# A decode attention kernel: K and V loaded as 2 MB transfers with 16 KB per partition, V one group behind K, and weights loaded in long rows

## The chip, the cores and the metric

The kernel runs on one core of one Trainium2 chip. The metric is the device time of one execution in microseconds (us), the median of several. The profile is one more execution, recorded by the hardware profiler; its span, from the first to the last instruction, is 1.7 to 2.1 us shorter than the device time.

Names: TensorE (PE) multiplies matrices, and PEld is its weight load; VectorE (DVE), ScalarE (ACT) and SyncE (SP) are the other engines used. SP issues all of the DMA transfers but the five (before) or two (after) of w1 and w2. The profile counts 16 DMA engines for the core. SBUF is the memory, here tiles of 128 partitions, that the transfers fill; PSUM is the memory that TensorE writes its results to. In the records a load of all 128 partitions has 16 completions; here it has landed when the last of them has come (in the kernel before, TensorE's first matmul on a chunk comes 0.05 us after it at the earliest). A "packet" is one record of the DMA trace; for these loads it is one contiguous row of one partition (33,280 packets of 8 KB for 260 loads of 128 partitions, before).

## The reference, cut to what matters

One token, decoded: grouped-query attention over a long cache plus a small feed-forward block (FFN), everything in bf16.

```python
# x: [1,1,512]; k_cache, v_cache: [1, 8, 65536, 128]; wq: [512, 4096]; wo: [4096, 512]
# w1: [512, 1792]; w2: [1792, 512]
xn = _layernorm(x)
q  = (xn @ wq).reshape(1, 1, 32, 128)            # 32 heads, 4 per K/V group
scores = einsum("bhqd,bhkd->bhqk", q, repeat(k_cache, 4)) * 128 ** -0.5
o  = einsum("bhqk,bhkd->bhqd", softmax(scores), repeat(v_cache, 4))
out = x + o.reshape(1, 1, 4096) @ wo + (gelu(xn @ w1 + b1) @ w2 + b2)
```

K and V are 8 groups of 16 MB each: 256 MB that are read once. With the weights, the profile counts 280.5 MB (of 10^6 bytes) read from HBM.

## The kernel before

A group has 16 chunks of 4096 tokens (1 MB, 8 KB per partition). For a K chunk TensorE transposes 32 tiles into PSUM, VectorE and ScalarE copy them to SBUF, and 32 narrow matmuls give the scores. When a group's scores are complete, its maximum is found and ScalarE runs four exps, one for each head. A V chunk costs 32 narrow matmuls. V runs two groups behind K. The kernel turns all tile dependencies into semaphore waits.

```python
    NB = 12                                    # chunk buffers of 1 MB
    cbuf = [nc.alloc_sbuf_tensor(f"cbuf{i}", [128, TPC, DH], BF) for i in range(NB)]
    ...
    VLAG = 2
    for ph in range(NPH):                      # a phase: chunks of K of group ph, V of group ph - VLAG
        ks = [("K", ph, c) for c in range(NCH)] if ph < G else []
        vs = [("V", ph - VLAG, c) for c in range(NCH)] if ph >= VLAG else []
        ...                                    # taken in turn: K, V, K, V
    def item_src(it):
        kind, g, c = it
        cache = A_k_cache if kind == "K" else A_v_cache
        return cache[0, g, c * CH:(c + 1) * CH, :].rearrange("(p t) d -> p t d", p=128)
    ...                                        # SP issues each chunk's load as soon as its buffer is free
    def dma_w12():                             # issued by ACT after the last K chunk
        for kt in range(KT):
            ... in_=B_w1[kt * 128:(kt + 1) * 128, :]                    # rows of 3.5 KB
        ... in_=B_w2.rearrange("(fc p) n -> p fc n", p=128)             # rows of 1 KB
        # one semaphore: a reader of w1 waits for w1 and w2
    ...
        else:                                  # a V chunk
            if softmax_q and softmax_group[0] == g:
                flush_softmax()
            gen_pv(g, c, b)
            ...
            if ph == last_phase and pos_in_phase >= 1:
                for _ in range(ffn_per_item):  # 2 pieces of the FFN per V chunk
                    if ffn_pieces: ffn_pieces.pop(0)()
```

Of the kernel before, what the change touches and what calls it, by code (L numbers as in the profile page):

```python
# [5 lines left out]
BF = mybir.dt.bfloat16  # L6
# [144 lines left out]
def bass_parallel_sum__gqa_block_cached__dense_activation_gelu__decode_kernel(  # L151
# [13 lines left out]
    D = A_x.shape[-1]  # L165
    DH = 128
    H = A_wq.shape[1] // DH
    G = A_k_cache.shape[1]
    HPG = H // G
    S = A_k_cache.shape[2]  # L170
    F = B_w1.shape[1]
    FC = F // 128
    KT = D // 128
# [6 lines left out]
    assert D % 128 == 0 and F % 128 == 0 and S % CH == 0 and NCH % 4 == 0  # L180
    assert A_k_cache.shape[3] == DH and H % G == 0 and KT == 4 and HPG == 4

    NB = 12
    NKT = 4
    NPT = 4
    NPS = 2
    LA = 2

    SCALE = 1.0 / math.sqrt(DH)
    EPS = 1e-5  # L190
# [35 lines left out]
    finT = nc.alloc_sbuf_tensor("finT", [128, KT], F32)  # L226
    fin4_bf = nc.alloc_sbuf_tensor("fin4_bf", [KT, 128], BF)

    cbuf = [nc.alloc_sbuf_tensor(f"cbuf{i}", [128, TPC, DH], BF) for i in range(NB)]
    assert NB >= KT + 4 and TPC * DH == H * DH  # L230
    WQ_SLOT0 = NB - KT
    wq_kt = [cbuf[WQ_SLOT0 + kt][:, :, :].rearrange("p t d -> p (t d)") for kt in range(KT)]
    assert CH * NKT >= KT * F + FC * D
    R_kt = nc.alloc_sbuf_tensor("R_kt", [128, NKT * CH], BF)
    ktbuf = [R_kt[:, i * CH:(i + 1) * CH] for i in range(NKT)]
# [3 lines left out]
    wo_g = [nc.alloc_sbuf_tensor(f"wo_g{i}", [128, HPG, D], BF) for i in range(2)]  # L239
    scf = [nc.alloc_sbuf_tensor(f"scf{i}", [128, TPG * HPG], F32) for i in range(2)]  # L240
    scf_v = [scf[i][:, :].rearrange("p (t j) -> p t j", j=HPG) for i in range(2)]
    P_bf = [nc.alloc_sbuf_tensor(f"P_bf{i}", [128, TPG * HPG], BF) for i in range(3)]
    P_v = [P_bf[i][:, :].rearrange("p (t j) -> p t j", j=HPG) for i in range(3)]

    pmax = [nc.alloc_sbuf_tensor(f"pmax{i}", [128, HPG], F32) for i in range(2)]
    pmax_parts = [nc.alloc_sbuf_tensor(f"pmax_parts{i}", [128, BPG * HPG], F32) for i in range(2)]
# [54 lines left out]
    sch.dma(SP, lambda: sp.dma_start(out=b2row_bf[:, :], in_=B_b2.rearrange("(o n) -> o n", o=1)),  # L301
            sem_misc, writes=["b2row"], total=48)

    VLAG = 2
    NPH = G + VLAG
    items = []
    phase_start = []
    for ph in range(NPH):
        ks = [("K", ph, c) for c in range(NCH)] if ph < G else []
        vs = [("V", ph - VLAG, c) for c in range(NCH)] if ph >= VLAG else []  # L310
        phase_start.append(len(items))
        seq = []
        for c in range(NCH):
            if ks:
                seq.append(ks[c])
            if vs:
                seq.append(vs[c])
        items.extend(seq)
    NITEMS = len(items)
    assert NITEMS == 2 * NKCH  # L320
    NPB = VLAG + 1

    def item_src(it):
        kind, g, c = it
        cache = A_k_cache if kind == "K" else A_v_cache
        return cache[0, g, c * CH:(c + 1) * CH, :].rearrange("(p t) d -> p t d", p=128)

    next_item = [0]
    dma_hooks = {}

    def dma_items_upto(n_excl):
        while next_item[0] < min(n_excl, NITEMS):
            n = next_item[0]
            b = n % NB
            src = item_src(items[n])
            sch.dma(SP, lambda b=b, src=src: sp.dma_start(out=cbuf[b][:, :, :], in_=src),
                    csem[b], writes=[f"cbuf{b}"])
            for h in dma_hooks.get(n, ()):
                h()
            next_item[0] += 1  # L340

    def dma_wq():
        for kt in range(KT):
            sch.dma(
                SP,
                lambda kt=kt: sp.dma_start(out=wq_kt[kt], in_=A_wq[kt * 128:(kt + 1) * 128, :]),  # L346
                sem_wq, writes=[f"cbuf{WQ_SLOT0 + kt}"], total=16 * KT,
            )

    wo_sems = [sch.dsem("dwo0"), sch.dsem("dwo1")]  # L350
# [8 lines left out]
        )  # L359

    def dma_w12():
        for kt in range(KT):
            sch.dma(
                ACT,
                lambda kt=kt: act.dma_start(out=w1_sb[:, kt, :], in_=B_w1[kt * 128:(kt + 1) * 128, :]),
                sem_w12, writes=["w1_sb"] + (KT_RES_ALL if kt == 0 else []), total=16 * (KT + 1),
            )
        sch.dma(ACT, lambda: act.dma_start(out=w2_sb[:, :, :],
                                          in_=B_w2.rearrange("(fc p) n -> p fc n", p=128)),
                sem_w12, writes=["w2_sb"], total=16 * (KT + 1))  # L370

    dma_hooks[1] = [dma_wq]

    sch.op(DVE, lambda: dve.tensor_copy(out=xrow_f[:, :], in_=xrow_bf[:, :]),
           reads=["xrow_bf"], writes=["xrow_f"])
# [29 lines left out]
    for kt in range(KT):  # L405
        sch.op(
            PE,
            lambda kt=kt: pe.matmul(pA[:, PA_XN + kt:PA_XN + kt + 1],  # L408
                                    lhsT=xn_row_bf[0:1, kt * 128:(kt + 1) * 128],
                                    rhs=ident_bf[0:1, 0:1], start=True, stop=True),  # L410
            reads=["xn_row", "ident_bf"], writes=["pA"], publish=(kt == KT - 1),
        )
# [3 lines left out]
    def dva_for_fill(n):  # L416
        return DVE if (n % 8) in (0, 2, 3, 5, 6) else ACT

    def gen_transposes(i, b):
        for t in range(TPC):  # L420
            tg = i * TPC + t
            nfill = tg // 8
            tb = nfill % NPT
            slot = tg % 8
            last_of_bank = slot == 7
            sch.op(
                PE,
                lambda tb=tb, slot=slot, b=b, t=t: pe.transpose(  # L428
                    pst[tb][:, slot * 128:(slot + 1) * 128], cbuf[b][:, t, :], ident_bf[:, :]
                ),  # L430
                reads=[f"cbuf{b}", "ident_bf"], writes=[f"pst{tb}"], publish=last_of_bank,
            )
            if last_of_bank:
                e = dva_for_fill(nfill)
                kb = i % NKT
                q = t // 8
                dst = ktbuf[kb][:, q * 1024:(q + 1) * 1024]
                if e is DVE:
                    fn = (lambda tb=tb, dst=dst: dve.tensor_copy(out=dst, in_=pst[tb][:, :]))  # L439
                else:  # L440
                    fn = (lambda tb=tb, dst=dst: act.activation(out=dst, in_=pst[tb][:, :],  # L441
                                                                func=ACTF.Copy))
                sch.op(e, fn, reads=[f"pst{tb}"], writes=[f"ktbuf{kb}_{q}"])
# [80 lines left out]

    def gen_exps(g, js):
        gp = g % 2
        gq = g % 3
        for j in js:
            sch.op(
                ACT,  # L530
                lambda gp=gp, gq=gq, g=g, j=j: act.activation(  # L531
                    out=P_v[gq][:, :, j], in_=scf_v[gp][:, :, j], func=ACTF.Exp,
                    bias=negm[gp][:, j:j + 1], scale=1.0,
                    accum_out=sums[:, g * HPG + j:g * HPG + j + 1],
                ),
                reads=[f"negm{gp}"] + [f"scf{gp}_{k}" for k in range(BPG)],
                writes=[f"P{gq}_{j}", f"sums{g}_{j}"],
            )

    def gen_pv(g, c, b):  # L540
        gp = g % 3
        for t in range(TPC):
            sch.op(
                PE,
                lambda g=g, c=c, b=b, t=t, gp=gp: pe.matmul(  # L545
                    pB[:, PB_O + g * HPG:PB_O + (g + 1) * HPG],
                    lhsT=cbuf[b][:, t, :],
                    rhs=P_v[gp][:, c * TPC + t, :],
                    start=(c == 0 and t == 0), stop=(c == NCH - 1 and t == TPC - 1),
                ),  # L550
                reads=[f"cbuf{b}"] + [f"P{gp}_{j}" for j in range(HPG)], writes=["pB"],
                publish=(t == TPC - 1),
            )

    def gen_qproj():
        for h in range(H):
            for kt in range(KT):
                sch.op(
                    PE,
                    lambda h=h, kt=kt: pe.matmul(  # L560
                        pA[:, PA_Q + h:PA_Q + h + 1],
                        lhsT=wq_kt[kt][:, h * DH:(h + 1) * DH],
                        rhs=xnT_bf[:, kt:kt + 1], start=(kt == 0), stop=(kt == KT - 1),
                    ),
                    reads=[f"cbuf{WQ_SLOT0 + kt}", "xnT"], writes=["pA"],
                    publish=(h == H - 1 and kt == KT - 1),
                )
        sch.op(
            DVE,
            lambda: dve.tensor_scalar(out=qT_bf[:, :], in0=pA[:, PA_Q:PA_Q + H], scalar1=SCALE,  # L570
                                      scalar2=None, op0=ALU.mult),
            reads=["pA"], writes=["qT"],
        )
# [40 lines left out]
    def gen_ffn1_piece(fc):  # L614
        if True:
            for kt in range(KT):
# [1 line left out]
                    PE,  # L618
                    lambda fc=fc, kt=kt: pe.matmul(
                        pA[:, PA_H + fc:PA_H + fc + 1],  # L620
                        lhsT=w1_sb[:, kt, fc * 128:(fc + 1) * 128],
                        rhs=xnT_bf[:, kt:kt + 1], start=(kt == 0), stop=False,
                    ),
                    reads=["w1_sb", "xnT"], writes=["pA"], publish=False,
# [2 lines left out]
                PE,  # L627
                lambda fc=fc: pe.matmul(  # L628
                    pA[:, PA_H + fc:PA_H + fc + 1],
                    lhsT=b1row_bf[0:1, fc * 128:(fc + 1) * 128],  # L630
                    rhs=ident_bf[0:1, 0:1], start=False, stop=True,
                ),
                reads=["b1row", "ident_bf"], writes=["pA"], publish=(fc == FC - 1),
# [68 lines left out]
    ffn_per_item = -(-len(ffn_pieces) // max(1, NCH - 3))  # L702

    def dma_cap(n):
        return n if qproj_done[0] else min(n, NB - KT)

    dma_items_upto(dma_cap(NB))

# [20 lines left out]

    for n, it in enumerate(items):  # L730
        kind, g, c = it
        b = n % NB
        ph = phase_of_item[n]
        pos_in_phase = n - phase_start[ph]
        if kind == "K":
            i = kcount
            kcount += 1
            had_pending = bool(softmax_q)
            gen_transposes(i, b)
            if i == min(1, NKCH - 1):  # L740
                gen_qproj()
                qproj_done[0] = True
# [12 lines left out]
        else:  # L755
            if softmax_q and softmax_group[0] == g:
                flush_softmax()
            gen_pv(g, c, b)
            while epi_q:
                epi_q.pop(0)()  # L760
            if c == NCH - 1:
# [5 lines left out]
                        ffn_pieces.pop(0)()  # L767
        if pos_in_phase == min(6, NCH - 1) and ph >= VLAG:
            dma_wo(ph - VLAG)
        dma_items_upto(dma_cap(n + NB + 1))  # L770
    flush_softmax()
    while ffn_pieces:
        ffn_pieces.pop(0)()
# [77 lines left out]
```

## Time and profile before

| | before |
|---|---|
| time, median of 3 (lowest to highest) | 699.86 us (699.52 to 699.91) |
| span of the profile | 698.1 us |
| DMA share, 20 to 600 us | 1.01 in each stretch of 100 us |
| rate in those stretches | 408 to 416 GB/s |
| TensorE busy | 559.7 us (80%) |
| last V transfer landed | 692.8 us |

From the page of the kernel before, the lines that say how full the DMA engines are. In the row `DMA` each digit is the busy share of a fortieth of the span in tenths, 9 for 90% or more; the row below it is the rate.

```profile
DMA  8999999999999999999999999999999999999993
GB/s 344 418 416 415 416 416 417 415 412 416 416 415 413 416 416 416 416 412 417 417 416 411 406 418 416 418 400 411 417 417 417 380 416 416 416 413 400 411 392 139
DMA packets 44170, 282.22 MB, mean 404 GB/s; under 512 B 4379, under 2 KB 10269, under 8 KB 10782
q1 hardware_dynamic: 41678, 276.85, 96.7%
q8 instruction: 100, 1.64, 1.0%
DMA 58%; PE 36%; issue 3%; ACT 1%; DVE 1%; SPq 0%
```

The engines are busy from the first fortieth to the last but one. `q8`, which the page calls "instruction", is the fetch of instructions: 100 packets of 16 KB, 1.07 us each. The last line is the chain of work that ended last, by engine; "issue" is time in which an engine waited for nothing that the profile shows.

From the timeline of the kernel before, the end of the run on TensorE (start us, busy us, in brackets the idle time before):

```profile
692.88 1.02 PE L545 MATMUL pB<-P_bf,cbuf 128*128 128x4 bf16 x32 [1.50 <-DMA cbuf<-in_A_v_cache_dram]
693.76 0.57 PE L579 MATMUL pA<-sums,ones_f 128*128 128x4 f32 x2
```

After the last landing there are 32 matmuls and a short fixed tail; 692.8 to 698.1 is 5.3 us.

The trace also has a record of every DMA packet. Medians by size, counted from those records for the kernel before:

```
     4 B    4375 packets  median 9 ns      (semaphore updates)
  1024 B    5890 packets  median 46 ns     (wo, w2)
  3584 B     513 packets  median 140 ns    (w1)
  8192 B   33280 packets  median 313 ns    (K, V, wq)
```

A straight line through 1024 B and 8192 B, with 309 ns for the latter (its median from 5 to 15 us), has a slope of 27.2 B/ns and leaves about 8.5 ns per packet that does not depend on its size.

### The profile page before, as it was taken

What the parts mean: (1) busy time and instruction counts of PE and PEld (TensorE: products, weight loads), DVE (VectorE), ACT (ScalarE), POOL (GpSimd) and SP (SyncE); (2) the same over time, 40 slices, a digit from 0 to 9 for tenths busy, and PEclk for the clock granted to TensorE, in tenths of its full rate; (3) what the DMA queues carried; (4) which work ended last, traced back from release to release, by engine and by line L of the source; (5) the groups of instructions that cost most, each with busy time, mean ns of one, the idle gap of its engine ahead of it and who ended that gap; (6) DMA issues with size and microseconds to landing.
All of it is one profiled execution on the core that took longest, in us unless ns stands there. A gap on an engine that the chain in (4) does not pass through costs nothing.

```text
span 698.1 us, 26642 instructions
## 1 busy us (share of the span) xinstructions
PE 559.7 (80%) x12732; PEld 544.6 (78%) x12732; DVE 281.0 (40%) x457; ACT 245.1 (35%) x266; POOL 1.3 (0%) x10
## 2 busy tenths in 40 slices
PE   3888888998898888978888888989889979733454
PEld 3888888888898888878888888888888878633453
DVE  2366765444454444433444344544344434200000
ACT  4344664362335332352324422253323433300000
POOL 0000000000000000000000000000000000000000
PEclk9799999696778898785888687785788588655555
DMA  8999999999999999999999999999999999999993
GB/s 344 418 416 415 416 416 417 415 412 416 416 415 413 416 416 416 416 412 417 417 416 411 406 418 416 418 400 411 417 417 417 380 416 416 416 413 400 411 392 139
DMA packets 44170, 282.22 MB, mean 404 GB/s; under 512 B 4379, under 2 KB 10269, under 8 KB 10782
## 3 DMA queue, kind: packets, MB, share of 16 engines
q1 hardware_dynamic: 41678, 276.85, 96.7%
q10 hardware_dynamic: 2384, 3.67, 1.4%
q8 instruction: 100, 1.64, 1.0%
q14 instruction: 8, 0.07, 0.0%
HBM read 280.50 MB, written 0.00 MB: 402 GB/s over the span
## 4 chain that ended last, share of the span: by engine, by line
DMA 58%; PE 36%; issue 3%; ACT 1%; DVE 1%; SPq 0%
DMA cbuf<-in_A_k_cache_dram 41%; PE pst L428 23%; DMA cbuf<-in_A_v_cache_dram 15%; PE pss L454 7%; PE pB L545 4%; DMA cbuf<-in_A_wq_dram 2%; PE pA L560 1%; ACT R_kt L441 0%; PE pA L599 0%; PE pA L492 0%; PE pA L514 0%; SPq L346 0%; ACT P_bf L531 0%; PE pA L579 0%; ACT L531 0%
## 5 line engine op out<-in xcount | busy, mean ns | idle before, releaser
L428 PE MATMUL pst<-ident_bf,cbuf 128*128 128x128 bf16 x4096 | 331.8, 254 | 53.4 <-DMA cbuf<-in_A_k_cache_dram 37.5
L428 PEld LDWEIGHTS pst<-ident_bf,cbuf 128*128 128x128 bf16 x4096 | 305.8, 117 | 63.5 <-issue 57.6
L441 ACT ACTIVATE R_kt<-pst 128x1024 bf16<-128x1024 bf16 x192 | 196.3, 1024 | 358.3 <-PE pst L428 358.1
L439 DVE COPY R_kt<-pst 128x1024 bf16<-128x1024 bf16 x320 | 212.9, 688 | 259.6 <-PE pst L428 259.1
L545 PE MATMUL pB<-P_bf,cbuf 128*128 128x4 bf16 x4096 | 125.7, 165 | 54.9 <-DMA cbuf<-in_A_v_cache_dram 43.5
L545 PEld LDWEIGHTS pB<-P_bf,cbuf 128*128 128x128 bf16 x4096 | 115.5, 99 | 57.0 <-DMA cbuf<-in_A_v_cache_dram 44.1
L454 PE MATMUL pss<-qT_bf,R_kt 128*128 128x4 bf16 x4096 | 124.4, 165 | 6.3 <-issue 6.2
L454 PEld LDWEIGHTS pss<-qT_bf,R_kt 128*128 128x128 bf16 x4096 | 121.2, 98 | 7.0 <-issue 7.0
L531 ACT ACTIVATE P_bf<-scf,negm 128x512 bf16<-128x512 f32 x32 | 45.6, 1445 | 5.5 <-DVE negm L520 5.5
L471 DVE TENSOR_REDUCE pmax_parts<-scf 128x4 f32<-128x512 f32 x32 | 34.1, 1066 | 1.1
L467 DVE COPY scf<-pss 128x512 f32<-128x512 f32 x32 | 22.1, 692 | 22.1 <-PE pss L454 22.1
L583 DVE RECIPROCAL rtot<-pA 128x4 f32<-128x4 f32 x8 | 1.5, 183 | 65.3 <-PE pA L579 65.3
L646 ACT ACTIVATE g_t<-g_t 128x14 f32<-128x14 f32 x1 | 0.2, 214 | 62.6 <-DVE g_t L644 62.6
L599 PE MATMUL pA<-oT_bf,wo_g 128*128 128x1 bf16 x128 | 4.5, 165 | 5.2 <-DMA wo_g<-in_A_wo_dram 4.7
L609 DVE TENSOR_TENSOR finT<-pA,finT 128x4 f32<-128x4 f32 x8 | 1.3, 163 | 18.1 <-PE pA L599 18.1
L531 ACT ACTIVATION_READ_ACCUMULATOR P_bf<-scf,negm 128x1 f32 x32 | 8.4, 263 | 0.0
L599 PEld LDWEIGHTS pA<-oT_bf,wo_g 128*128 128x128 bf16 x128 | 4.0, 102 | 5.4 <-DMA wo_g<-in_A_wo_dram 4.8
L560 PE MATMUL pA<-xnT_bf,cbuf 128*128 128x1 bf16 x128 | 3.6, 165 | 5.1 <-DMA cbuf<-in_A_wq_dram 5.1
L560 PEld LDWEIGHTS pA<-xnT_bf,cbuf 128*128 128x128 bf16 x128 | 3.5, 104 | 5.3 <-DMA cbuf<-in_A_wq_dram 5.3
L637 DVE COPY h_f<-pA 128x14 f32<-128x14 f32 x1 | 0.2, 174 | 15.7 <-PE pA L628 15.7
L408 PE MATMUL pA<-ident_bf,xn_row_bf 1*128 1x1 bf16 x4 | 0.3, 164 | 7.6 <-ACT xn_row_bf L401 7.6
L408 PEld LDWEIGHTS pA<-ident_bf,xn_row_bf 1*128 1x128 bf16 x4 | 0.2, 101 | 7.6 <-ACT xn_row_bf L401 7.6
(62 smaller groups left out, 53.5 us busy)
## 6 DMA issues: line engine op xcount, KB each, us to landing
cbuf<-in_A_k_cache_dram SPq DMA_DIRECT2D x128, 1024.0 KB, 23.9
cbuf<-in_A_v_cache_dram SPq DMA_DIRECT2D x128, 1024.0 KB, 26.9
cbuf<-in_A_wq_dram SPq DMA_DIRECT2D x4, 1024.0 KB, 11.9
wo_g<-in_A_wo_dram SPq DMA_DIRECT2D x8, 512.0 KB, 27.0
R_kt<-in_B_w_dram ACTq DMA_DIRECT2D x4, 448.0 KB, 14.0
R_kt<-in_B_w_dram ACTq DMA_DIRECT2D x1, 1792.0 KB, 48.4
xrow_bf<-in_A_x_dram SPq DMA_DIRECT2D x1, 1.0 KB
b1row_bf<-in_B_b_dram SPq DMA_DIRECT2D x1, 3.5 KB
```

The costliest lines, as they stand in the source:

```text
L428: lambda tb=tb, slot=slot, b=b, t=t: pe.transpose(pst[tb][:, slot * 128:(slot + 1) * 128], cbuf[b][:, t, :], ident_bf[:, :]),
L439: fn = (lambda tb=tb, dst=dst: dve.tensor_copy(out=dst, in_=pst[tb][:, :]))
L441: fn = (lambda tb=tb, dst=dst: act.activation(out=dst, in_=pst[tb][:, :], func=ACTF.Copy))
L454: lambda sb=sb, slot=slot, kb=kb, t=t, g=g: pe.matmul(pss[sb][:, slot * HPG:(slot + 1) * HPG], lhsT=ktbuf[kb][:, t * 128:(t + 1) * 128], r ...
L467: sch.op(DVE, lambda sb=sb, dst=dst: dve.tensor_copy(out=dst, in_=pss[sb][:, :]), reads=[f"pss{sb}"], writes=[f"scf{gp}_{k4}"])
L471: lambda gp=gp, k4=k4, dst=dst: dve.tensor_reduce(out=pmax_parts[gp][:, k4 * HPG:(k4 + 1) * HPG], in_=dst.rearrange("p (t j) -> p j t", j= ...
L531: lambda gp=gp, gq=gq, g=g, j=j: act.activation(out=P_v[gq][:, :, j], in_=scf_v[gp][:, :, j], func=ACTF.Exp, bias=negm[gp][:, j:j + 1], sc ...
L545: lambda g=g, c=c, b=b, t=t, gp=gp: pe.matmul(pB[:, PB_O + g * HPG:PB_O + (g + 1) * HPG], lhsT=cbuf[b][:, t, :], rhs=P_v[gp][:, c * TPC + ...
L560: lambda h=h, kt=kt: pe.matmul(pA[:, PA_Q + h:PA_Q + h + 1], lhsT=wq_kt[kt][:, h * DH:(h + 1) * DH], rhs=xnT_bf[:, kt:kt + 1], start=(kt = ...
L583: sch.op(DVE, lambda hs=hs: dve.reciprocal(out=rtot[:, hs], in_=pA[:, PA_SUM:PA_SUM + HPG]), reads=["pA"], writes=[f"rtot{g}"])
L599: lambda kt=kt, j=j, h=h, g=g: pe.matmul(pA[:, PA_AT + kt:PA_AT + kt + 1], lhsT=wo_g[g % 2][:, j, kt * 128:(kt + 1) * 128], rhs=oT_bf[:, h ...
L609: lambda: dve.tensor_tensor(out=finT[:, :], in0=pA[:, PA_AT:PA_AT + KT], in1=finT[:, :], op=ALU.add),
```

## The change

The intent: K and V come in transfers of 2 MB whose rows are 16 KB per partition, in 8 buffers of 2 MB. V is one group behind K instead of two. The weights wq, w1 and w2 are laid out so that a partition reads one long row: partition p holds rows 4p to 4p+3 of w1 and rows 14p to 14p+13 of w2. For that, w1's columns are read by the matmuls with a step of 14 elements (28 bytes).

```diff
-    NB = 12
+    NSUB = 2
+    TPD = NSUB * TPC
+    NB = 8
...
+    VLAG = 1
+    NPB = VLAG + 1
...
-    cbuf = [nc.alloc_sbuf_tensor(f"cbuf{i}", [128, TPC, DH], BF) for i in range(NB)]
+    call = nc.alloc_sbuf_tensor("cbuf", [128, NB * TPD * DH], BF)
+    cbuf = [call[:, i * TPD * DH:(i + 1) * TPD * DH].rearrange("p (t d) -> p t d", d=DH)
+            for i in range(NB)]
...
+        for c in range(0, NCH + NSUB, NSUB):          # K K, then V V
+            if ph < G and c < NCH:
+                items.extend(("K", ph, c + s) for s in range(NSUB))
+            if ph >= VLAG and c >= NSUB:
+                items.extend(("V", ph - VLAG, c - NSUB + s) for s in range(NSUB))
...
-        return cache[0, g, c * CH:(c + 1) * CH, :].rearrange("(p t) d -> p t d", p=128)
+        return cache[0, g, c * CH:(c + NSUB) * CH, :].rearrange("(p t) d -> p t d", p=128)
...
-        for kt in range(KT):
-            sch.dma(
-                ACT,
-                lambda kt=kt: act.dma_start(out=w1_sb[:, kt, :], in_=B_w1[kt * 128:(kt + 1) * 128, :]),
-                sem_w12, writes=["w1_sb"] + (KT_RES_ALL if kt == 0 else []), total=16 * (KT + 1),
-            )
+        sch.dma(ACT, lambda: act.dma_start(out=w1_sb[:, :, :],
+                                          in_=B_w1.rearrange("(p kt) f -> p kt f", kt=KT)),
+                sem_w12, writes=["w1_sb"] + KT_RES_ALL, total=32)
         sch.dma(ACT, lambda: act.dma_start(out=w2_sb[:, :, :],
-                                          in_=B_w2.rearrange("(fc p) n -> p fc n", p=128)),
-                sem_w12, writes=["w2_sb"], total=16 * (KT + 1))
+                                          in_=B_w2.rearrange("(p fc) n -> p fc n", fc=FC)),
+                sem_w12, writes=["w2_sb"], total=32)
...
-                        lhsT=w1_sb[:, kt, fc * 128:(fc + 1) * 128],
+                        lhsT=w1_sb[:, kt, fc:F:FC],
...                    # wq, xn and b1 are permuted in the same way; cut
```

More of the change, by code (lines that the diff above doesn't have):

```diff
@@ L227, in bass_parallel_sum__gqa_block_cached__dense_activation_gelu__decode_kernel @@
     fin4_bf = nc.alloc_sbuf_tensor("fin4_bf", [KT, 128], BF)
-    cbuf = [nc.alloc_sbuf_tensor(f"cbuf{i}", [128, TPC, DH], BF) for i in range(NB)]
-    assert NB >= KT + 4 and TPC * DH == H * DH
-    WQ_SLOT0 = NB - KT
-    wq_kt = [cbuf[WQ_SLOT0 + kt][:, :, :].rearrange("p t d -> p (t d)") for kt in range(KT)]
+    call = nc.alloc_sbuf_tensor("cbuf", [128, NB * TPD * DH], BF)
+    cbuf = [call[:, i * TPD * DH:(i + 1) * TPD * DH].rearrange("p (t d) -> p t d", d=DH)
+            for i in range(NB)]
+    assert KT % NSUB == 0 and TPC * DH == H * DH
+    NWQ = KT // NSUB
+    WQ_SLOT0 = NB - NWQ
+    wq_kt = [call[:, (WQ_SLOT0 * NSUB + kt) * TPC * DH:(WQ_SLOT0 * NSUB + kt + 1) * TPC * DH]
+             for kt in range(KT)]
+    wq_slot = [WQ_SLOT0 + kt // NSUB for kt in range(KT)]
     assert CH * NKT >= KT * F + FC * D
@@ L241, in bass_parallel_sum__gqa_block_cached__dense_activation_gelu__decode_kernel @@
     scf_v = [scf[i][:, :].rearrange("p (t j) -> p t j", j=HPG) for i in range(2)]
-    P_bf = [nc.alloc_sbuf_tensor(f"P_bf{i}", [128, TPG * HPG], BF) for i in range(3)]
-    P_v = [P_bf[i][:, :].rearrange("p (t j) -> p t j", j=HPG) for i in range(3)]
+    P_bf = [nc.alloc_sbuf_tensor(f"P_bf{i}", [128, TPG * HPG], BF) for i in range(NPB)]
+    P_v = [P_bf[i][:, :].rearrange("p (t j) -> p t j", j=HPG) for i in range(NPB)]
     pmax = [nc.alloc_sbuf_tensor(f"pmax{i}", [128, HPG], F32) for i in range(2)]
@@ L302, in bass_parallel_sum__gqa_block_cached__dense_activation_gelu__decode_kernel @@
             sem_misc, writes=["b2row"], total=48)
-    VLAG = 2
     NPH = G + VLAG
@@ L308, in bass_parallel_sum__gqa_block_cached__dense_activation_gelu__decode_kernel @@
     for ph in range(NPH):
-        ks = [("K", ph, c) for c in range(NCH)] if ph < G else []
-        vs = [("V", ph - VLAG, c) for c in range(NCH)] if ph >= VLAG else []
         phase_start.append(len(items))
-        seq = []
-        for c in range(NCH):
-            if ks:
-                seq.append(ks[c])
-            if vs:
-                seq.append(vs[c])
-        items.extend(seq)
+        for c in range(0, NCH + NSUB, NSUB):
[3 more added lines that the diff above has]
+                items.extend(("V", ph - VLAG, c - NSUB + s) for s in range(NSUB))
     NITEMS = len(items)
     assert NITEMS == 2 * NKCH
-    NPB = VLAG + 1
     def item_src(it):
@@ L331, in dma_items_upto @@
     def dma_items_upto(n_excl):
-        while next_item[0] < min(n_excl, NITEMS):
+        while next_item[0] < min(n_excl, NITEMS // NSUB):
             n = next_item[0]
             b = n % NB
-            src = item_src(items[n])
+            src = item_src(items[n * NSUB])
             sch.dma(SP, lambda b=b, src=src: sp.dma_start(out=cbuf[b][:, :, :], in_=src),
@@ L342, in dma_wq @@
     def dma_wq():
-        for kt in range(KT):
+        wq_src = A_wq.rearrange("(p kt) n -> p kt n", kt=KT)
+        for w in range(NWQ):
+            dst = cbuf[WQ_SLOT0 + w].rearrange("p t d -> p (t d)").rearrange("p (k n) -> p k n", k=NSUB)
             sch.dma(
                 SP,
-                lambda kt=kt: sp.dma_start(out=wq_kt[kt], in_=A_wq[kt * 128:(kt + 1) * 128, :]),
-                sem_wq, writes=[f"cbuf{WQ_SLOT0 + kt}"], total=16 * KT,
+                lambda w=w, dst=dst: sp.dma_start(out=dst, in_=wq_src[:, w * NSUB:(w + 1) * NSUB, :]),
+                sem_wq, writes=[f"cbuf{WQ_SLOT0 + w}"], total=16 * NWQ,
             )
@@ L361, in dma_w12 @@
     def dma_w12():
-        for kt in range(KT):
-            sch.dma(
-                ACT,
-                lambda kt=kt: act.dma_start(out=w1_sb[:, kt, :], in_=B_w1[kt * 128:(kt + 1) * 128, :]),
-                sem_w12, writes=["w1_sb"] + (KT_RES_ALL if kt == 0 else []), total=16 * (KT + 1),
-            )
+        sch.dma(ACT, lambda: act.dma_start(out=w1_sb[:, :, :],
+                                          in_=B_w1.rearrange("(p kt) f -> p kt f", kt=KT)),
+                sem_w12, writes=["w1_sb"] + KT_RES_ALL, total=32)
         sch.dma(ACT, lambda: act.dma_start(out=w2_sb[:, :, :],
-                                          in_=B_w2.rearrange("(fc p) n -> p fc n", p=128)),
-                sem_w12, writes=["w2_sb"], total=16 * (KT + 1))
-    dma_hooks[1] = [dma_wq]
+                                          in_=B_w2.rearrange("(p fc) n -> p fc n", fc=FC)),
+                sem_w12, writes=["w2_sb"], total=32)
+    dma_hooks[0] = [dma_wq]
     sch.op(DVE, lambda: dve.tensor_copy(out=xrow_f[:, :], in_=xrow_bf[:, :]),
@@ L408, in bass_parallel_sum__gqa_block_cached__dense_activation_gelu__decode_kernel @@
             lambda kt=kt: pe.matmul(pA[:, PA_XN + kt:PA_XN + kt + 1],
-                                    lhsT=xn_row_bf[0:1, kt * 128:(kt + 1) * 128],
+                                    lhsT=xn_row_bf[0:1, kt:D:KT],
                                     rhs=ident_bf[0:1, 0:1], start=True, stop=True),
@@ L417, in dva_for_fill, with gen_transposes @@
         return DVE if (n % 8) in (0, 2, 3, 5, 6) else ACT
-    def gen_transposes(i, b):
+    def gen_transposes(i, b, u):
         for t in range(TPC):
@@ L427, in gen_transposes @@
                 PE,
-                lambda tb=tb, slot=slot, b=b, t=t: pe.transpose(
-                    pst[tb][:, slot * 128:(slot + 1) * 128], cbuf[b][:, t, :], ident_bf[:, :]
+                lambda tb=tb, slot=slot, b=b, t=t, u=u: pe.transpose(
+                    pst[tb][:, slot * 128:(slot + 1) * 128], cbuf[b][:, u + t, :], ident_bf[:, :]
                 ),
@@ L526, in gen_exps @@
         gp = g % 2
-        gq = g % 3
+        gq = g % NPB
         for j in js:
@@ L538, in gen_exps, with gen_pv @@
             )
-    def gen_pv(g, c, b):
-        gp = g % 3
+    def gen_pv(g, c, b, u):
+        gp = g % NPB
         for t in range(TPC):
@@ L544, in gen_pv @@
                 PE,
-                lambda g=g, c=c, b=b, t=t, gp=gp: pe.matmul(
+                lambda g=g, c=c, b=b, t=t, gp=gp, u=u: pe.matmul(
                     pB[:, PB_O + g * HPG:PB_O + (g + 1) * HPG],
-                    lhsT=cbuf[b][:, t, :],
+                    lhsT=cbuf[b][:, u + t, :],
                     rhs=P_v[gp][:, c * TPC + t, :],
@@ L564, in gen_qproj @@
                     ),
-                    reads=[f"cbuf{WQ_SLOT0 + kt}", "xnT"], writes=["pA"],
+                    reads=[f"cbuf{wq_slot[kt]}", "xnT"], writes=["pA"],
                     publish=(h == H - 1 and kt == KT - 1),
@@ L629, in gen_ffn1_piece @@
                     pA[:, PA_H + fc:PA_H + fc + 1],
-                    lhsT=b1row_bf[0:1, fc * 128:(fc + 1) * 128],
+                    lhsT=b1row_bf[0:1, fc:F:FC],
                     rhs=ident_bf[0:1, 0:1], start=False, stop=True,
@@ L704, in dma_cap @@
     def dma_cap(n):
-        return n if qproj_done[0] else min(n, NB - KT)
+        return n if qproj_done[0] else min(n, NB - NWQ)
     dma_items_upto(dma_cap(NB))
@@ L731, in bass_parallel_sum__gqa_block_cached__dense_activation_gelu__decode_kernel @@
         kind, g, c = it
-        b = n % NB
+        b = (n // NSUB) % NB
+        u = (n % NSUB) * TPC
         ph = phase_of_item[n]
@@ L738, in bass_parallel_sum__gqa_block_cached__dense_activation_gelu__decode_kernel @@
             had_pending = bool(softmax_q)
-            gen_transposes(i, b)
+            gen_transposes(i, b, u)
             if i == min(1, NKCH - 1):
@@ L757, in bass_parallel_sum__gqa_block_cached__dense_activation_gelu__decode_kernel @@
                 flush_softmax()
-            gen_pv(g, c, b)
+            gen_pv(g, c, b, u)
             while epi_q:
@@ L769, in bass_parallel_sum__gqa_block_cached__dense_activation_gelu__decode_kernel @@
             dma_wo(ph - VLAG)
-        dma_items_upto(dma_cap(n + NB + 1))
+        dma_items_upto(dma_cap((n + 1) // NSUB + NB))
     flush_softmax()
```

## The prediction

> **What bounds the kernel now: the DMA engines' own time.** The windows view has the DMA share at 1.00 to 1.03 in every stretch from 20 to 660 us, at 410 to 417 GB/s. The chain of waits is 58% DMA; TensorE's longest single wait is 2.9 us for K, 2.6 for V. The DMA table moves 282 MB; at 416 GB/s that is 678 of 698 us.
>
> The trace's packet records say where the rest of the rate goes. Median packet: 4 B 9 ns, 1024 B 46 ns, 3584 B 140 ns, 8192 B 313 ns (309 where nothing else runs): 27.2 B/ns plus about 8.5 ns per packet. A 1 MB transfer is 8 packets and one 4-byte semaphore packet on each engine: 8 x 310 + 9 = 2.49 us, as landings confirm. [...]
>
> Instruction fetch (100 packets of 16 KB, 1.07 us each) repeats with a period of 8[...]; the 16 completions of a transfer spread from 0.5 to 15 us over the run, and the last 15 us run at half share. The late half sets the time.
>
> **Removed.** Per 2 MB, each engine saves 8 packet overheads and one semaphore packet, 77 ns; 128 K/V plus 2 wq transfers: 10.0 us. w1 and w2 go from 144 packets per engine to 16: 1.1 us. Sum 11 us, all on the critical resource.
>
> **Added.**
> 1. The last buffer carries two chunks of V: 32 more matmuls after the last landing, +0.9 us.
> 2. With V one group behind, the first V of a group forces four exps (1.24 us apart) at once: TensorE stalls about 5 us per group. A K+V pair costs TensorE about 4.2 us (two chunks of K alone 6.2, with a 0.84 us "issue" gap that looks like instruction fetch) against 4.9 us of DMA. 16 pairs and the stall are 74 to 79 us against 80 us of DMA per group: TensorE is nearly a second bottleneck; 16 MB of buffers hide its lag.
> 3. The end is tighter: only one V-only group. The w1/w2 load starts after the last K and shares the engines with V; I estimate 18 to 20 us, landing near 655 us. TensorE waits for it, then has the FFN and 15 chunks of V left, some 22 us.
> 4. 56 weight loads read w1 with a 28-byte stride. [...]
>
> **Sum.** DMA alone: 699.9 - 11.1 + 0.9 = 689.7. For the tail (3 and 4) I add about 2: **691.5 us**, range 684 to 704 (8 in 10). Faster by over 2%: 0.10; within 2%: 0.83; slower: 0.07.
>
> **Right or wrong by:** 16 KB packets near 610 ns, 2 MB landings every 4.90 us; steady rate near 422 GB/s; about 20,000 packets fewer; TensorE's waits for K mostly gone in the middle; about 5 us of waiting for exps at each group; last V landing near 682 us; strided w1 loads longer than 97 ns.
>
> **What would break it:** 16 KB packets with no lower cost per byte (no gain); instruction fetch slower behind longer packets, so that TensorE's lag empties the queue (700 to 715 us); a longer wait for w1/w2.

The sum came to 691.5 us: 699.9 less 11.1, plus 0.9 for the last chunk, plus about 2 for the tail (3 and 4). The 18 to 20 us of term 3 agree with the packet records of the kernel before: 16 rows of 14 KB per engine, 536 ns each by the line above, in turn with as many of 16 KB at 611 ns make 18.4 us. The load took 23.5 us (635.2 to 658.7 us).

## More of the kernel before

From the groups of instructions of the kernel before, with shapes kept apart: busy us, mean ns of one | idle us just before them, and what ended it.

```profile
L428 PE MATMUL pst<-ident_bf,cbuf 128*128 128x128 bf16 x4096 | 331.8, 254 | 53.4 <-DMA cbuf<-in_A_k_cache_dram 37.5 <-issue 12.9 <-ACT R_kt L441 1.3
L545 PE MATMUL pB<-P_bf,cbuf 128*128 128x4 bf16 x4096 | 125.7, 165 | 54.9 <-DMA cbuf<-in_A_v_cache_dram 43.5 <-issue 10.9 <-DVE oT_bf L587 0.5
L619 PEld LDWEIGHTS pA<-xnT_bf,R_kt 128*128 128x128 bf16 x56 | 2.6, 106 | 0.1
```

TensorE waits 37.5 us for K and 43.5 us for V.

## The result, and the profile after

| | before | after |
|---|---|---|
| time, median (lowest to highest), 4 executions each | 699.83 us (699.52 to 699.91) | 690.28 us (689.21 to 690.61) |
| ratio, 95% interval | | 0.9862 (0.9848 to 0.9876) |
| span of the profile | 698.1 us | 688.1 us |
| rate, 20 to 600 us, in stretches of 100 us | 408 to 416 GB/s | 422 to 423 GB/s |
| last V transfer landed | 692.8 us | 680.8 us |
| from there to the end of the span | 5.3 us | 7.3 us |

A ratio is the mean time of one kernel's fast runs over that of the other's fast runs of the same rounds, so it is not quite the ratio of the medians. The change is 1.4% faster, below the 2% at which a difference is called faster.

The span shrank by 10.0 us: the last V landed 12.0 us earlier, and the tail behind it grew by 2.0 us. From the page of the changed kernel:

```profile
DMA  8999999999999999999999999999999999999972
GB/s 345 426 426 422 424 423 418 422 427 424 423 416 424 425 422 418 423 424 424 424 417 426 422 424 420 418 426 424 427 418 422 421 425 425 421 424 421 425 310 110
DMA packets 23352, 282.19 MB, mean 410 GB/s; under 512 B 2251, under 2 KB 6349, under 8 KB 6350
q1 hardware_dynamic: 22958, 276.84, 95.7%
q8 instruction: 99, 1.62, 1.0%
PE 64%; DMA 21%; issue 7%; ACT 6%; DVE 1%; SPq 0%
```

From the windows of both kernels, one stretch of 100 us each, before and then after (the last three numbers are the granted TensorE clock, the DMA share and GB/s):

```profile
120.00:220.00 100.00, 92.14 (x2062) 90.43 (x2059) 46.10 (x75) 40.16 (x43) 0.00 (x0) 0.76 1.01 415
120.00:220.00 100.00, 83.41 (x1936) 81.89 (x1935) 42.91 (x67) 35.27 (x38) 0.00 (x0) 0.79 1.01 423
```

The same bytes come in 20,818 packets fewer, and the rate is higher all along. The chain of waits has turned from 58% DMA to 64% TensorE. Read alone, it would say that TensorE is now the bottleneck. The rows above it say otherwise: the DMA engines are as full as before. TensorE is late: it starts on a transfer 7.2 us after its landing in the median and 17.5 at most, where landings are 4.90 us apart (before: 1.4 us in the median). So it rarely waits for data (9.5 us for K in all); the chain follows TensorE, and the transfers run ahead of it at 422 to 423 GB/s. The experiments `rows8k` and `vlag2` below settle which reading is right.

From the groups of the changed kernel:

```profile
L430 PE MATMUL pst<-ident_bf,cbuf 128*128 128x128 bf16 x4096 | 319.7, 249 | 39.0 <-issue 28.2 <-DMA cbuf<-in_A_k_cache_dram 9.5 <-ACT R_kt L443 1.1
L547 PE MATMUL pB<-P_bf,cbuf 128*128 128x4 bf16 x4096 | 117.5, 165 | 60.3 <-ACT P_bf L533 38.7 <-issue 21.6
L621 PEld LDWEIGHTS pA<-xnT_bf,R_kt 128*128 128x128 bf16 x56 | 4.4, 153 | 16.0 <-issue 15.9
```

TensorE's waits for K fell from 37.5 to 9.5 us, those for V are gone, and a wait for the exps (`P_bf`) of 38.7 us in 7 places is new, 5.5 us for each group. The strided loads of w1 take 153 ns on average, 106 before.

Packet medians of the changed kernel, from its records: 16384 B 614 ns (16640 packets), 14336 B 539 ns (256), 1024 B 46 ns, 4 B 9 ns. Two packets of 8 KB take 2 x 313 = 626 ns, 12 more. Transfers of 2 MB mostly land 4.90 us apart; two of 1 MB took 4.98.

The tail, from the chain of work that ended last, in order of time (start us, us, what):

```profile
635.65 23.04 DMA R_kt<-in_B_w_dram
658.83 0.37 PE pA L621 x4
...
677.01 1.51 PE pB L547 x53
678.52 2.39 issue
680.91 2.99 PE pB L547 x107
683.91 0.44 PE pA L581 x2
```

The load of w1 and w2 was issued at 635.2 us and landed at 658.7; TensorE stood still for it for 15.9 us and then had 14 chunks of V and the FFN to do. When the last V landed at 680.8 us it had nearly caught up, but it had been halted inside a chunk since 678.5 us, by nothing that the profile shows as a wait ("issue"). So 107 matmuls were left at 680.9 us instead of the 64 of the last buffer.

What goes before the end of such a halt can be read from the packet records. An instruction-fetch packet starts at 678.4 us, 2.6 us before this halt ends. After the first 25 us the change has 49 "issue" gaps of over 0.3 us before matmuls, 62 us in sum; 48 of them end 2.3 to 2.6 us after a fetch packet starts. In the kernel before it is all 34 (30 us in sum, 2.3 to 2.7 us after). Fetch packets come about 6 us apart, and only 4 to 6% of all matmuls start at that distance from one; of the gaps that a DMA ended, 1 of 64 does. So these halts go with instruction fetch, though no run changed the fetch.

### The profile page after: what moved, and what is told of

Its sections match the earlier page's. It is cut to its first block, busy times and chain, and to the rows that moved or that the text cites. A ratio compares the mean times of both kernels' runs of the same rounds, so it can differ in the third digit from the quotient of the medians.

```text
span 688.1 us, 26439 instructions
## 1 busy us (share of the span) xinstructions
PE 542.2 (79%) x12732; PEld 531.3 (77%) x12732; DVE 280.9 (41%) x457; ACT 243.9 (35%) x266; POOL 1.3 (0%) x10
## 4 chain that ended last, share of the span: by engine, by line
PE 64%; DMA 21%; issue 7%; ACT 6%; DVE 1%; SPq 0%
PE pst L430 37%; DMA cbuf<-in_A_k_cache_dram 18%; PE pss L456 12%; PE pB L547 12%; ACT P_bf L533 5%; DMA R_kt<-in_B_w_dram 3%; PE pA L621 1%; PE pA L601 0%; PE pA L494 0%; PE pA L516 0%; PE pA L630 0%; ACT R_kt L443 0%; DVE R_kt L441 0%; PE pA L581 0%; PE pA L661 0%
## 5 line engine op out<-in xcount | busy, mean ns | idle before, releaser
L430 PE MATMUL pst<-ident_bf,cbuf 128*128 128x128 bf16 x4096 | 319.7, 249 | 39.0 <-issue 28.2
L443 ACT ACTIVATE R_kt<-pst 128x1024 bf16<-128x1024 bf16 x192 | 196.6, 1024 | 387.4 <-PE pst L430 387.4
L430 PEld LDWEIGHTS pst<-ident_bf,cbuf 128*128 128x128 bf16 x4096 | 294.2, 114 | 44.6 <-issue 40.1
L547 PE MATMUL pB<-P_bf,cbuf 128*128 128x4 bf16 x4096 | 117.5, 165 | 60.3 <-ACT P_bf L533 38.7
L547 PEld LDWEIGHTS pB<-P_bf,cbuf 128*128 128x128 bf16 x4096 | 111.5, 99 | 62.4 <-ACT P_bf L533 39.3
L533 ACT ACTIVATE P_bf<-scf,negm 128x512 bf16<-128x512 f32 x32 | 40.8, 1424 | 6.9 <-DVE negm L522 6.9
L621 PE MATMUL pA<-xnT_bf,R_kt 128*128 128x1 bf16 x56 | 5.4, 201 | 15.9 <-DMA R_kt<-in_B_w_dram 15.9
L621 PEld LDWEIGHTS pA<-xnT_bf,R_kt 128*128 128x128 bf16 x56 | 4.4, 153 | 16.0 <-issue 15.9
(58 smaller groups left out, 57.6 us busy)
```

The source lines that it names most:

```text
L430: lambda tb=tb, slot=slot, b=b, t=t, u=u: pe.transpose(pst[tb][:, slot * 128:(slot + 1) * 128], cbuf[b][:, u + t, :], ident_bf[:, :]),
L443: fn = (lambda tb=tb, dst=dst: act.activation(out=dst, in_=pst[tb][:, :], func=ACTF.Copy))
L533: lambda gp=gp, gq=gq, g=g, j=j: act.activation(out=P_v[gq][:, :, j], in_=scf_v[gp][:, :, j], func=ACTF.Exp, bias=negm[gp][:, j:j + 1], sc ...
L547: lambda g=g, c=c, b=b, t=t, gp=gp, u=u: pe.matmul(pB[:, PB_O + g * HPG:PB_O + (g + 1) * HPG], lhsT=cbuf[b][:, u + t, :], rhs=P_v[gp][:, c ...
L621: lambda fc=fc, kt=kt: pe.matmul(pA[:, PA_H + fc:PA_H + fc + 1], lhsT=w1_sb[:, kt, fc:F:FC], rhs=xnT_bf[:, kt:kt + 1], start=(kt == 0), st ...
```

## The experiments

Twelve variants ran, all with correct results, each in three timed rounds beside the kernel before. The median of before was 699.76 us in the first set of four, 699.88 in the second and 699.84 in the third.

| kernel | time, us (lowest to highest) | ratio to before |
|---|---|---|
| the change | 690.28 (689.21 to 690.61) | 0.9862 |
| rows8k | 699.31 (699.13 to 700.34) | 0.9997 |
| before4k | 715.05 (714.98 to 715.14) | 1.0218 |
| rows32k | 689.65 (688.14 to 692.74) | 0.9861 |
| wlong | 698.62 (698.38 to 698.65) | 0.9982 |
| only2mb | 698.48 (698.40 to 698.80) | 0.9983 |
| oldw | 707.97 (707.63 to 708.81) | 1.0119 |
| vlag2 | 688.95 (688.83 to 689.27) | 0.9846 |
| ffnlate | 688.58 (688.44 to 689.12) | 0.9841 |
| best16 | 689.72 (688.56 to 689.83) | 0.9852 |
| best32 | 691.29 (690.61 to 693.08) | 0.9882 |
| wo8 | 716.47 (716.04 to 718.10) | 1.0236 |
| shift | 909.43 (897.58 to 928.59) | 1.2863 |

### rows8k: the same transfers, in rows of 8 KB

```diff
-        return cache[0, g, c * CH:(c + NSUB) * CH, :].rearrange("(p t) d -> p t d", p=128)
+        return cache[0, g, c * CH:(c + NSUB) * CH, :].rearrange("(s p t) d -> p s (t d)", p=128, s=NSUB)
```

> The changed kernel, but each 2 MB K/V transfer is made of two runs of 8 KB per partition instead of one of 16 KB; transfers, buffers, order and semaphores stay. Packet theory (a fixed cost of about 8.5 ns per packet): 128 x 8 x 8.5 ns = 8.7 us come back, about 699.0 us; 8 KB packets of 313 ns, 2 MB landings every 4.97 us. Rival (fewer and larger transfers, half as many semaphores and issues, is what pays): stays at 690.3 within 1.5 us.

Measured: 699.31 us. The whole gain is gone, though the transfers are still 2 MB, with half as many semaphores and issues, in the same buffers and order. The 8 KB packets are back at 313 ns and the landings at 4.98 us. This rules out the size of the transfer and the number of transfers as causes, and leaves the length of the row. What the cost of a row consists of, the runs do not show.

It also answers the question about the chain of waits. The chain of this kernel is 55% TensorE and 33% DMA, and yet slower packets alone cost 9.0 us:

```profile
GB/s 345 416 417 415 418 417 414 418 416 417 414 414 418 416 417 412 416 417 418 418 410 417 418 418 413 406 418 417 418 395 397 417 418 418 393 415 415 422 381 129
PE 55%; DMA 33%; ACT 6%; issue 5%; DVE 1%; SPq 0%
```

### before4k: the kernel before, in rows of 4 KB

```diff
-        return cache[0, g, c * CH:(c + 1) * CH, :].rearrange("(p t) d -> p t d", p=128)
+        return cache[0, g, c * CH:(c + 1) * CH, :].rearrange("(s p t) d -> p s (t d)", p=128, s=2)
```

> The kernel before with each 1 MB K/V transfer made of two runs of 4 KB per partition instead of one of 8 KB; nothing else. Packet theory: 256 transfers x 8 more packets x 8.5 ns = 17.4 us more, 717.2 us, within 2; 4 KB packets of about 159 ns. Rival (cost goes by bytes or by transfers): 699.8 within 1.5.

Measured: 715.05 us, 15.2 us more than before. That is 2048 more packets per engine at 7.4 ns each; the expected 8.5 ns was 2.2 us too much. The 4 KB packets took 162 ns. Together with rows8k (9.0 us for 1024 packets per engine, 8.8 ns each), the cost per packet is 7 to 9 ns of the kernel's time from 4 to 16 KB. The packet records alone would say 11 to 12 ns (2 x 162 - 313, 2 x 313 - 614).

### wlong and only2mb: the parts alone

wlong is the kernel before with only the new layout of the weights. only2mb is the change without it for w1 and w2, and with V two groups behind. V two groups behind takes a third buffer for the exps (4096 bytes per partition); to make room for it, these kernels have one wo buffer.

```diff
 # wlong: dma_w12 and the reads of w1, b1 as in the change; K/V, buffers and VLAG as before
 # only2mb: the change, and
-    VLAG = 1
+    VLAG = 2
-    wo_g = [nc.alloc_sbuf_tensor(f"wo_g{i}", [128, HPG, D], BF) for i in range(2)]
+    wo_g = [nc.alloc_sbuf_tensor("wo_g0", [128, HPG, D], BF)] * 2
 # and w1 in four loads of B_w1[kt:D:KT, :], w2 as "(fc p) n -> p fc n", columns of w1 without a stride
```

> The changed kernel with V two groups behind K and w1/w2 as before (wo in one buffer, to make room): of the change, only the 2 MB transfers of 16 KB rows and the 16 MB of buffers are left. Packet theory: before minus 10.0 plus 0.9 = 690.7 us, within 1.5. Rival (the distance of V, or the layout of the weights, carries the gain): 695 to 700 us.

Measured: 698.48 us, a miss by 8 us. The reason is in its trace. The last V landed at 680.5 us, as in the changed kernel: the data did come faster. But w2 landed only at 671.7 us, and TensorE had most of the last group's V still to do. From its waits (us in total, times, longest) and its DMA issues (count, size, us from issue to landing):

```profile
PE pA L624 <- DMA R_kt<-in_B_w_dram: 15.8, 1, 15.8
...
R_kt<-in_B_w_dram ACTq DMA_DIRECT2D x4, 448.0 KB, 19.6
R_kt<-in_B_w_dram ACTq DMA_DIRECT2D x1, 1792.0 KB, 78.1
```

w2 took 78.1 us from issue to landing. For the first 26 us it stood behind w1 in the same queue; its first row moved at 619.5 us. Its rows are 1 KB, 112 per engine. The records show w2 and V keeping step, one record for one: from 622 to 630 and from 639 to 648 us, where no rows of wo pass, 454 rows of w2 stand beside 402 rows of V and the 53 semaphore packets of V's queue (455). In the kernel before, from 625 to 635 us, it is 486 records of the weights' queue beside 486 of V's. So in these stretches there was a record of V's queue, nearly always a row, for each row of w2: 614 ns with rows of 16 KB and 313 ns with rows of 8 KB. In the kernel before w2 landed 48.4 us after its issue.

> The kernel before with only the weights' layout of the change: w1 and w2 in one transfer each, rows of 14 KB, w1 read with a stride; K/V transfers, buffers and distance as before. Packet theory: 128 packets fewer per engine, -1.1 us: 698.7 within 0.7. With only2mb (698.5) this makes the two parts worth about 1.3 and 1.1 us alone and 10.9 together (vlag2 689.0): neither pays alone, because short packets of w2 taking turns with long packets of V are what eats the gain. Rival (the layout is worth 9 us by itself): 690 to 692.

Measured: 698.62 us, as expected.

### oldw: the change without the weights' layout

```diff
 # dma_w12 and the reads of w1, b1 as in only2mb; V one group behind, as in the change
```

> The changed kernel with w1/w2 loaded as before (w1 in rows of 3.5 KB in four transfers, w2 in rows of 1 KB; columns read without a stride). If the weights' layout is worth only its packets: 690.3 + 1.1 = 691.4 us. My theory: 112 packets of 1 KB per engine take turns with 16 KB packets of V, so w2 lands only when V has run out, near 683 us, and TensorE then still has the FFN and 15 chunks of V, some 22 us: 705 to 712 us.

Measured: 707.97 us. All transfers had landed by 681.8 us, and TensorE then worked for 24 us alone. It had waited 38.1 us:

```profile
PE pA L624 <- DMA R_kt<-in_B_w_dram: 38.1, 1, 38.1
```

So the weights' rows are worth 1.2 us alone and 17.7 us inside the change (707.97 - 690.28). The long rows of V made the short rows beside them slow (w2 took 78.1 us under only2mb, where the counts are, and 48.4 us before), and V one group behind leaves one V-only group, not two, to hide that.

### vlag2: V two groups behind

```diff
-    VLAG = 1
+    VLAG = 2
 # and one wo buffer
```

> The changed kernel with V two groups behind K (wo in one buffer, to make room). Theory (DMA bound, TensorE's waits hidden): 690.3 within 1.5 us, although the 39 us of waits for exps and the 15.9 us wait for w1/w2 go away. Rival (one group of distance costs time through those waits): 2 to 5 us faster. Rival (the shorter distance is part of the gain): 2 us or more slower.

Measured: 688.95 us, 1.3 us faster than the change, at the edge of what was expected (the 95% intervals of the two overlap). The waits for exps and the wait for w1/w2 are gone (w1 and w2 took 19.0 us to land, well ahead of their use), and the last V landed at the same 680.8 us. So these waits are not the bottleneck. The 1.3 us are in the tail: the "issue" halt of 2.39 us happened 1.5 us earlier here, so that it was over before the last landing:

```profile
679.40 3.36 PE L547 MATMUL pB<-P_bf,cbuf 128*128 128x4 bf16 x110 [2.39 <-issue]
```

From the landing to the end of the span it is 6.2 us. vlag2 and only2mb differ in the layout of w1 and w2 alone, and their times by 9.5 us.

### ffnlate: the FFN later

```diff
-    ffn_per_item = -(-len(ffn_pieces) // max(1, NCH - 3))
+    ffn_per_item = -(-len(ffn_pieces) // max(1, NCH - 9))
-            if ph == last_phase and pos_in_phase >= 1:
+            if ph == last_phase and pos_in_phase >= 6:
```

> The changed kernel with the FFN's pieces from the sixth V chunk of the last group on instead of the second, three to a chunk. Theory (the 15.9 us wait for w1/w2 is behind DMA): the wait shrinks below 5 us or goes, the time stays at 690.3 within 1.2. Rival (the wait sets the end): 2 to 5 us faster.

Measured: 688.58 us (in the edit the pieces start with the seventh V chunk), 1.7 us faster, more than the theory allowed and less than the rival asked. The wait for w1/w2 shrank to 2.8 us. The end of the run, on TensorE, in its timeline:

```profile
677.80 1.01 PE L547 MATMUL pB<-P_bf,cbuf 128*128 128x4 bf16 x32
680.52 1.87 PE L547 MATMUL pB<-P_bf,cbuf 128*128 128x4 bf16 x64 [1.70 <-DMA cbuf<-in_A_v_cache_dram]
682.25 0.57 PE L581 MATMUL pA<-sums,ones_f 128*128 128x4 f32 x2
```

TensorE was idle when the last V landed (680.5 us), did the 64 matmuls and ended: 6.1 us from the landing to the end of the span, against 7.3 in the change. That is 5.3 as before plus 0.8 for 32 more matmuls. But the "issue" halt that stood in the tail of the change is gone from there too. So the wait for w1/w2, which made TensorE late, and the halt together cost the change about 1.2 us, through work that was left over at the end, and not the wait's 15.9 us; their shares were not separated. In vlag2, without the wait, a halt of the same length cost nothing. ffnlate is the fastest kernel, though its interval (0.9827 to 0.9856) overlaps that of the change.

### rows32k and best32: rows of 32 KB

```diff
-    NSUB = 2
+    NSUB = 4
-    NB = 8
+    NB = 4
 # best32 has VLAG = 2 with one wo buffer besides, and the last 4 MB of V as four transfers
```

> The changed kernel with 4 MB transfers of 32 KB per partition in 4 buffers (16 MB as before). Packet theory: per 4 MB, 8 packets and one semaphore packet fewer, 77 ns x 65 = 5.0 us less, but 64 more matmuls after the last landing, +1.9: 687 us; 32 KB packets of 1.22 us. If four buffers are too coarse, TensorE's pauses empty the queue and the time is 692 to 705, with the DMA share below 1.00 in the middle of the run. Rival (no packet above 16 KB): 691 to 693.

Measured: 689.65 us, with a wider scatter, where 687 was expected. The 32 KB packets took 1216 ns, 12 less than two of 16 KB, the landings of 4 MB were 9.73 us apart against 2 x 4.90, and the last V landed at 673.9 us, 6.9 us earlier than in the change. The time did not follow. TensorE waited 16.6 us for w1/w2 and was still working when the data had long ended:

```profile
679.17 4.67 PE L547 MATMUL pB<-P_bf,cbuf 128*128 128x4 bf16 x160
683.71 0.57 PE L581 MATMUL pA<-sums,ones_f 128*128 128x4 f32 x2
```

Here the wait for w1/w2 has become part of the end of the run: the chain of work that ended last goes back along TensorE to that landing.

> rows32k with V two groups behind (wo in one buffer) and the last 4 MB of V as four transfers of 1 MB. In rows32k the last V landed at 673.9 us, 6.9 before the changed kernel's, but TensorE, held up by the wait for w1/w2, ended no earlier. If so, with that wait out of the way the time is 681.5 within 2. Rival (32 KB packets give nothing; DMA ends the run at the same time): 688 to 691.

Measured: 691.29 us, a miss by 10 us, and close to the rival's number, though not for the rival's reason: the 32 KB packets again took 1215 ns. The wait for w1/w2 is gone, but the DMA engines ran dry earlier. Its stretches, with the busy time of PE, PEld, DVE, ACT and POOL, then granted clock, DMA share and GB/s:

```profile
80.00:100.00 20.00, 19.19 (x444) 18.58 (x443) 14.52 (x26) 15.33 (x18) 0.00 (x0) 0.98 1.00 426
100.00:120.00 20.00, 17.50 (x370) 17.16 (x368) 11.57 (x17) 9.52 (x11) 0.00 (x0) 0.83 0.84 338
120.00:140.00 20.00, 16.97 (x400) 16.23 (x397) 13.72 (x22) 9.75 (x10) 0.00 (x0) 1.00 0.83 332
```

With V two groups behind, the first two groups are K alone, where TensorE needs about 3.1 us a chunk and DMA delivers one in 2.45; with four buffers of 4 MB the lag of TensorE probably reaches all of them. That is argued, not tested; vlag2, with the same 16 MB in eight buffers, shows no such dip. The combination of rows of 32 KB, V one group behind and a later FFN was not run; whether it is faster is open.

### best16: the last 2 MB of V in two transfers

```diff
+            if n == NITEMS // NSUB - 1:
+                for s in range(NSUB):
+                    ts = slice(s * TPC, (s + 1) * TPC)
+                    ...  # out=cbuf[b][:, ts, :], in_=src[:, ts, :], a semaphore and a tile name each
 # on top of vlag2
```

> vlag2 with the last 2 MB of V as two transfers of 1 MB with a semaphore each, so that 32 matmuls and not 64 stand after the last landing: the +0.9 us of the tail is given back: 688.1 within 0.8.

Measured: 689.72 us, not 0.9 us faster than vlag2: a miss. (It is 0.8 slower, which is not clear of the noise.) The profile again has an "issue" halt inside the last chunks, until 680.70 us, with 110 matmuls left; the last V landed at 681.4 us, and the split could have left 32 after it. The halt, not the granularity of the last transfer, sets the tail in this profile:

```profile
680.70 3.07 PE L555 MATMUL pB<-P_bf,cbuf 128*128 128x4 bf16 x110 [2.12 <-issue]
```

### wo8 and shift: is one half of the DMA engines late?

The 16 completions of a transfer lie within 0.5 us (before) or 0.9 us (after) at the start of the run and within 15 us (before) or 21 us (after) at the end. I guessed that instruction fetch makes one half of the engines late, and tried to move work between the halves. That 8 engines take a transfer of 8 partitions is supported by the count of completions in wo8, 896 more than in vlag2: 128 transfers with 8 each in place of 8 with 16. Which engines they were, no record here tells. The 11.9 us in wo8's are an estimate: wo is 4096 rows of 1 KB, 256 per engine, at about 46 ns.

```diff
 # wo8: vlag2, and each wo load as 16 transfers of 8 partitions
+      for e in range(16):
...
+                out=wo_g[g % 2][e * 8:(e + 1) * 8, :, :],
 # shift: vlag2, and in every eighth K/V transfer
+            parts = ((0, 112), (112, 120), (120, 128)) if n % 8 == 3 else ((0, 128),)
```

> vlag2, but each wo load is 16 transfers of 8 partitions. If those run on 8 of the 16 engines[...], these 8 spend 11.9 us more over the run and the other 8 spend 11.9 us less. Theory (one half of the engines ends 15 to 20 us late and sets the time): either these are the early half, then the completions close up to under 10 us and the time is 681 to 685 us, or they are the late half, then the spread grows to 40 us and the time is 699 to 702. Rival (the spread doesn't matter, or the transfers still use 16 engines): 689 within 1.5.

Measured: 716.47 us, which none of the theories allowed. The completions did close up, to 4 to 6 us in the last transfers. From the timeline of SP's queue:

```profile
377.33 0.33 SPq L339 DMA_DIRECT2D cbuf<-in_A_v_cache_dram  x1
377.70 32.06 SPq L361 DMA_DIRECT2D wo_g<-in_A_wo_dram  x16
409.81 0.35 SPq L339 DMA_DIRECT2D cbuf<-in_A_k_cache_dram  x1
```

The issue of 16 small transfers behind the queued K/V loads took 32 us. No K/V load was issued meanwhile, and the queue drained (DMA share 0.73 from 400 to 410 us). That the completions closed up because all engines met at the empty queue is my reading of it. The test says nothing about the halves.

> vlag2, but in 16 of the 128 K/V transfers partitions 0 to 111 go in one transfer and the last 16 in two of 8 partitions each[...]. Theory (one half of the engines is late by 15 to 20 us[...] and sets the time): [...] Rival (the spread doesn't set the time): 689 within 1.5.

Measured: 909.43 us. Two of its four executions, the profiled one among them, are over 1.5% above its fastest run. Its 16 KB packets took 799 ns on average against 620 in vlag2. The loss comes in stretches; each of the first five split transfers, to 260 us, is followed by one. From 120 to 140 us the rate is 246 GB/s at a DMA share of 1.02, in the 20 us before and after it 421 and 415. So the splitting is its cause; whether it is the 112 partitions, and how, is not known. This test is inconclusive too.

The kept traces show the two halves themselves: in the change, eight of the 16 completions of the last transfer lie within 4.4 us of the first and the other eight 18.7 to 20.7 us behind it, and the DMA share is 0.51 from 664 to 676 us. In the kernel before it is 1.8 us for the first eight and 13.4 to 15.3 us for the others. That the late half is late because of instruction fetch was not shown.

## Why the prediction was right, point by point

- **Bound by the DMA engines' time: shown.** The share stayed at 1.01 in both kernels (from 20 to 600 us), and rows8k and before4k moved the time by row length alone.
- **11 us removed (10.0 from K, V and wq, 1.1 from w1 and w2): about right.** rows8k gives back 9.0 us, where 8.7 were expected for K and V; wlong gains 1.2. The last V landed 12.0 us earlier; the remaining 0.9 us were not traced. The predicted marks came: 16 KB packets of 614 ns (610), landings every 4.90 us (4.90), about 423 GB/s (422), 20,818 packets fewer (20,000), last V at 680.8 us (682).
- **One more chunk after the last landing, +0.9 us: shown** by ffnlate, where the tail is 6.1 us instead of 5.3.
- **Stall of about 5 us for the exps at each group, hidden by the buffers: shown.** 38.7 us in 7 places; vlag2 has none and is 1.3 us faster, all of it in the tail.
- **w1/w2 landing near 655 us, with 22 us of work behind it, for about 2 us: right in kind, a little large.** It landed at 658.7 us and cost about 1.2 us, together with the "issue" halt in the tail (change against ffnlate). The strided weight loads took 0.05 us more each (153 ns, 106 before), some 2.6 us for all 56, and how much of that reached the end was not measured.
- **What the prediction did not see.** It put the weights' layout down at 1.1 us. That is its worth alone. In the presence of 16 KB rows it decides whether there is a gain at all: without it the change loses 8.2 us to before (oldw), and even with V two groups behind nearly all of the gain is lost (only2mb).
- **How much the number proves.** The sum was 1.2 us too high. Its two errors point the same way, about 0.9 us more removed and 0.9 less added (2.0 instead of 2.9), so neither hid the other. But the range of 684 to 704 would have held with no gain at all; it is the marks and the experiments that carry the case. That the change contained the weights' layout, on which its gain hangs, was luck as far as the prediction goes.
- **The warning about instruction fetch behind longer packets was not borne out.** PEld's "issue" gaps before transposes are 1.43 us on average in the change (40.1 us in 28) and 1.40 in rows8k (47.6 in 34), so they were the same with rows of 16 and of 8 KB. In the kernel before they were 1.05 (57.6 in 55); why, was not tested.

## What to carry to other kernels

When the DMA share stands at 1, as here, look at the packet records: in these runs each row cost 7 to 9 ns of the kernel's time beyond its bytes, and longer rows, not larger transfers, saved it (rows8k: 9.0 us). Before making the rows of one stream longer, look at what shares the engines with it, because in these runs a stream of short rows got one row for each record of the other queue (486 beside 486) and w2 took 78.1 us to land beside rows of 16 KB, 48.4 beside rows of 8 KB; with long rows for w1 and w2 too, the two landed in 19.0 us (vlag2). And a chain of waits that ran 55% along TensorE did not prove TensorE the bottleneck in rows8k, where the DMA engines were busy for 90% or more of all fortieths but the first and the last: slower packets alone cost 9.0 us there.
